# Head weights in two transfers of uneven shape, and a last weighing in another order, in a two-layer decode kernel

## The chip, the cores and the metric

The kernel runs on one core of a Trainium2 chip. The metric is device time in microseconds of one execution, as the median of several runs. Tensor, vector and scalar work run on TensorE (PE, with its weight loads as PEld), VectorE (DVE), ScalarE (ACT) and GpSimd (POOL); SyncE (SP) does nothing here but issue transfers. All transfers from memory run on the core's 16 DMA engines; each of them works through a ring of its own, in the order in which SP issued.

## The reference

One token for each of two batch entries goes twice through an attention block with cached keys and values and a gated FFN, all in 32-bit floats:

```python
B, D, H, Sk, Dh, F = 2, 448, 16, 4096, 256, 1792
def _A_ref(x, k_cache, v_cache, wq, wo):
    q = (x @ wq)                                    # per head: 448 -> 256
    scores = einsum("bhqd,bhkd->bhqk", q, k_cache) * Dh ** -0.5
    p = softmax(scores)
    o = einsum("bhqk,bhkd->bhqd", p, v_cache)
    return o.reshape(B, 1, H * Dh) @ wo
def _B_ref(x, W_gate, W_up, W_down):
    h = relu(x @ W_gate) * (x @ W_up)
    return h @ W_down
x = x + A(layernorm(x)); x = x + B(layernorm(x))
x = x + A(layernorm(x)); x = x + B(layernorm(x))    # the same weights and caches again
```

The caches are 128 MiB each for keys and values and are read for both layers; nearly all the bytes are theirs.

## The kernel before, in words

**Units and memory.** A unit is one head of one batch entry: 4 MB of keys and 4 MB of values, each cut into four pieces of 1 MB (`NC` = 4). The first attention goes through 32 units, the second through the same in reverse. Nearly all of on-chip memory is one `arena` of 27 slots of 1 MB: six blocks of four slots for keys and values, three single slots, mostly for head weights. Twenty-two pieces and one head that the first attention read last are kept for the second.

**Loads.** `loads`, `cut` and `grouped` write out one list of transfers (`pending`): per pair of units k, v, k, the next head's weights, v; then seven pieces of `w_in` and four of `w_out` for the FFN. `pump` issues them on SP in that order as soon as a slot is free; `release` frees a slot when its last product is recorded, and calls `pump`. In the middle, keys and values go as one transfer of 4 MB. Eight semaphores serve the transfers in turn, so that each issue also waits for the eighth transfer before it. A head's weights are one transfer of 128 rows of 7168 bytes: three stretches of 256 columns for rows 0 to 383 of wq, 128 columns that hold wq's last 64 rows (`TAIL`) for both halves of the head on the two halves of the partitions, and wo.

**Attention.** For a unit u, `score` multiplies each key piece by the query into the PSUM bank `raw`; `score_copy`, `score_turn`, `softmax_max` and `softmax_exp` make `probs`, with DVE, PE, POOL and ACT in turn; `weigh` multiplies each value piece by `probs` into `poa` or `pob`, in turn; `out_copy` (ACT) and `out_add` (DVE) make `row`; `out_turn` turns it with a product by ones, `out_keep` (DVE) stores it as `oT`, and `project` adds the head's share of the output to the bank `y`. `query` makes q for the next two units. PE runs what is recorded in the order of the code:

```python
for u in range(n_u - 1):
    scores(u)
    if u % 2: query(u + 1)
    if u < n_u - 2: outputs(u)
u = n_u - 1            # score, turn and softmax of the last unit, then:
outputs(u - 1)
out_turn(u - 1)
out_keep(u - 1)
outputs(u)             # weigh 0..3, softmax_sum, out_copy
```

`outputs(u)` is the four steps of `weigh`, `softmax_sum`, `out_copy` and, but for the last unit, `out_add`. `row` is one buffer: the last `out_copy` may write it only after the `out_turn` of the unit before. `busy(n, half)` issues n products of the identity with itself into a bank that nobody reads; they keep PE at work where it would wait.

**FFN.** `absorb` adds up `y` and turns it, `squares`, `deviation` and `inverse` make the layer norm's factor; `proj` goes through the pieces of `w_in` for gate and up, the loop over j through those of `w_out`, with one `busy` product behind some of them.

Of the kernel before, what the change touches and what calls it, by code (L numbers as in the profile page):

```python
# [14 lines left out]
B, D, H, S, DH, F = 2, 448, 16, 4096, 256, 1792  # L15
P = 128
DC = 5
FULL, TAIL = 3, 64
NT = S // P
CT = 8  # L20
UNIT = CT * DH
NC = NT // CT
BLOCKS, SINGLES = 6, 3
KEPT = 22
# [41 lines left out]
def two_layers(  # L66
# [3 lines left out]
    k_cache: bass.AP,  # L70
    v_cache: bass.AP,
    w_head: bass.AP,
    w_in: bass.AP,
    w_out: bass.AP,
    out: bass.AP,
):
    nc = tc.nc
# [34 lines left out]
    def pump():  # L112
        while pending:
            at = None
            for i, ((kind, name, c), n) in enumerate(pending[: AHEAD if pending[0][1] == 1 else 1]):
                if i and kind != "h":
                    continue
                last = at_of.get((kind, name, c - 1)) if kind in "kv" else None
                at = units.take(n, kind, last)
                if at is not None:  # L120
                    break
            if at is None:
                return
            pending.pop(i)
            src = source((kind, name, c), n)
            dst = arena[:, at * UNIT : at * UNIT + src.shape[1]]
            parts = [0, src.shape[1]]
            if kind == "v" and n == 1 and c == NC - 1 and name in (first[-1], second[-1]):
                parts[1:1] = [UNIT // 2]
            if not pending:  # L130
                parts[1:1] = [src.shape[1] - D]
            for i, j in zip(parts, parts[1:]):
                nc.sync.dma_start(dst[:, i:j], src[:, i:j])
            for k in range(n):
                at_of[kind, name, c + k] = at + k

    def get(*key):
        at = at_of[key]
        return arena[:, at * UNIT : (at + 1) * UNIT]

# [77 lines left out]
    xT = xr[:, :, :, 0]  # L218
# [18 lines left out]
    def busy(n, half):  # L237

        for _ in range(n):
            nc.tensor.matmul(  # L240
                po_all[half][:B, :DH], ident[:, :B],
                ident[:, None, :].to_broadcast([P, 2, P]), start=True, stop=True,
            )
# [47 lines left out]
    def attention(order, after):  # L291
# [8 lines left out]
        def query(u):  # L300
            h = order[u][0]
            w = get("h", h, 0)
            pq = pq_all
            for j in range(2):
                if j and u == 0:
                    again()
                for c in range(FULL):
                    at = c * DH + j * P
                    nc.tensor.matmul(  # L309
                        pq[:, j, :], w[:, at : at + P], xT[:, c, :], start=(c == 0), stop=False  # L310
                    )
                nc.tensor.matmul(  # L312
                    pq[:, j, :], w[:, FULL * DH : FULL * DH + P], xT[:, FULL + j, :],
                    start=False, stop=True,
                )
            q = q_pad[:, u // 2 % 2]
            nc.vector.tensor_copy(q[..., 1], pq)
            for v in (u, u + 1):
                q_of[v] = q[:, :, order[v][1]]
# [56 lines left out]
        def weigh(u, c):  # L376


            vt = get("v", order[u], c)
            if c == 0:  # L380
                po_of[u] = po_all[u % 2]
            for t in range(CT if u == n_u - 1 else 0):
                n = c * CT + t
                nc.tensor.matmul(
                    po_of[u][32 * (t % 4) : 32 * (t % 4) + 1, :DH],
                    p_of[u][:, n : n + 1],
                    vt[:, t * DH : (t + 1) * DH],
                    start=(c == 0 and t < 4),
                    stop=(c == NC - 1 and t >= 4),
                )  # L390
            for t in range(CT // 2 if u < n_u - 1 else 0):
                n = c * CT + 2 * t
                nc.tensor.matmul(  # L393
                    po_of[u][32 * t : 32 * t + 2, :],
                    p_of[u][:, n : n + 2],
                    vt[:, 2 * t * DH : (2 * t + 2) * DH],
                    start=(c == 0),
                    stop=(c == NC - 1),
                )
            if ("v", order[u], c) not in after:  # L400
                release("v", order[u], c)
            if u == n_u - 1 and 0 < c < NC - 1:
                busy(2, (u + 1) % 2)

        def out_copy(u):
            nc.scalar.activation(row[:, :DH], po_of[u][:, :DH], AF.Copy, scale=r_of[u][:, 0:1])  # L406
# [9 lines left out]
        def out_turn(u):  # L416
            pT_of[u] = ps_s.tile([P, 2], F32, name="small")
            for c in range(2):
                nc.tensor.matmul(  # L419
                    pT_of[u][:, c : c + 1], row[:, c * P : (c + 1) * P], ones,  # L420
                    start=True, stop=True,
                )

        def out_keep(u):
            h, b = order[u]
            if h not in oT_of:
                oT_of[h] = work.tile([P, 2, B], F32, name="oT")
            nc.vector.tensor_copy(oT_of[h][:, :, b], pT_of.pop(u))  # L428

        def project(u):  # L430
            h = order[u][0]
            if u % 2 == 0:
                return
            wo = get("h", h, 0)[:, FULL * DH + P :]
            for c in range(2):
                add(
                    c, oT_of[h][:, c, :], wo[:, c * D : (c + 1) * D],
                    start=(c == 1 and u == 1), stop=(u == n_u - 1),
                )
            if ("h", h, 0) not in after:  # L440
                release("h", h, 0)
            if u == n_u - 1:
                busy(1, 0)
# [24 lines left out]
        def outputs(u):  # L468
            for c in range(NC):
                weigh(u, c)  # L470
            softmax_sum(u)
            out_copy(u)
            out_add(u)
# [12 lines left out]
        softmax_max(u)  # L486
        softmax_exp(u)
        outputs(u - 1)
        out_turn(u - 1)
        out_keep(u - 1)  # L490
        outputs(u)
        busy(1, 0)
        out_turn(u)
        out_keep(u)
        project(u)

    def ffn(last):
# [65 lines left out]
        for j in range(4):  # L563
            w = get("out", "", j)
            first_k = (14 * j + 2) // 4
            for k in range(first_k, (14 * j + 16) // 4):
                w_k = w[:, (k - first_k) * D : (k - first_k + 1) * D]
                if last and k == 13:
                    for half in range(2):
                        n = D - DH if half else DH  # L570
                        nc.tensor.matmul(
                            y[32 * half : 32 * half + B, :n],
                            ident[64:, 64 + 32 * half : 64 + 32 * half + B],
                            yrow[64:, :n], start=False, stop=False,
                        )
                add(
                    0 if last and k > 10 else k % 2, stat[k], w_k, (y, other)[k % 2 if k <= 10 else 0],
                    start=(k == 1), stop=(k in ((9, 13) if last else (12, 13))),
                )
            release("out", "", j)  # L580
            if last and j == 2:
                nc.scalar.activation(yrow[64:], other[64:, :DH], AF.Copy)
            if j < 2 or not last:
                busy(1, 0)

    add(0, ident[:B, :B], row[:B, :D], start=True, stop=True)
    absorb()
# [14 lines left out]
def _arrays(np, A_x, A_k_cache, A_v_cache, A_wq, A_wo, B_W_gate, B_W_up, B_W_down, **_):  # L602

    rows = FULL * P
    wq = A_wq.reshape(D, H, DH)
    head = [wq[c * P : (c + 1) * P].transpose(1, 0, 2) for c in range(FULL)]
    head.append(wq[rows:].reshape(TAIL, H, 2, P).transpose(1, 2, 0, 3).reshape(H, P, P))
    wo = A_wo.reshape(H, 2, P, D)
    head += [wo[:, 0], wo[:, 1]]
    full = [w[c * P : (c + 1) * P] for w in (B_W_gate, B_W_up) for c in range(FULL)]  # L610
    full.insert(FULL, np.concatenate([B_W_gate[rows:], B_W_up[rows:]]))
    down = B_W_down.reshape(4, D, D)
    chunks = [down[j, m * P : (m + 1) * P] for j in range(4) for m in range(FULL)]
    chunks += [np.concatenate([down[j, rows:], down[j + 1, rows:]]) for j in (0, 2)]
    k = A_k_cache.reshape(B, H, P, 2, E, G, 2, P).transpose(0, 1, 7, 3, 6, 5, 4, 2)
    found = {
        "x": A_x,
        "k_cache": k.reshape(B, H, P, S * 2),
        "v_cache": A_v_cache,
        "w_head": np.concatenate(head, axis=2),  # L620
        "w_in": np.stack(full),
        "w_out": np.concatenate(chunks, axis=1),
    }
    return {n: np.ascontiguousarray(a) for n, a in found.items()}
# [24 lines left out]
```

## Time and profile before

| | |
|---|---|
| median of 3 runs | 1327.57 us (1326.64 to 1327.68) |
| the profiled execution | 1328.09 us, its span 1326.3 us |
| mean granted TensorE clock | 0.761 |
| bytes moved | 562.42 MB, mean 424 GB/s |
| PE busy, PEld, DVE, ACT, POOL | 956.7, 322.8, 134.8, 92.0, 47.7 us |

The span runs from the first instruction to the last; the execution's own time holds 1.8 us more. A DMA share of 1.00 is all 16 engines at work; it can come out a little over 1 in a short stretch, since the records of two rows overlap by some nanoseconds. The first attention goes to about 670 us, the first FFN to 691, the second attention to 1305, the last FFN to the end.

### The profile page before, as it was taken

To read this page: it belongs to the slowest core of one execution; us is meant where nothing else is said; L and a number is where in the kernel's file an instruction comes from. 1 tells how busy PE (TensorE), PEld (TensorE's weight loads), DVE (VectorE), ACT (ScalarE), POOL (GpSimd) and SP (SyncE) were. 2 spreads that over 40 slices of the span, in tenths; PEclk is the share of its full clock that TensorE was granted. 3 is DMA by queue.
4 is the path that set the end of the run, shared out by engine and by line. 5 is a ranking of instruction groups with operands and counts; after the bars stand their busy time and mean duration, and the time that the engine had idled before them with its cause. 6 is when DMAs were issued, how large, how long until landed. Compare 5 with 4: busy or idle time off the path is not lost.

```text
span 1326.3 us, 13786 instructions
## 1 busy us (share of the span) xinstructions
PE 956.7 (72%) x6076; PEld 322.8 (24%) x6076; DVE 134.8 (10%) x457; ACT 92.0 (7%) x280; POOL 47.7 (4%) x134
## 2 busy tenths in 40 slices
PE   4767677877777766767788867777676676766678
PEld 2222123231232212222243322222122221222213
DVE  1101011010110100000101111010010100101100
ACT  1000000000000000000011100000000000000001
POOL 0000000000000000000000000000000000000000
PEclk9777766667767777686798897776777777778779
DMA  9999999999999999999999999999999999999997
GB/s 403 427 433 428 432 428 436 425 434 426 427 436 430 430 429 426 434 428 432 421 368 391 434 431 430 432 429 431 430 430 429 432 428 433 429 432 430 428 423 324
DMA packets 28152, 562.42 MB, mean 424 GB/s; under 512 B 3126, under 2 KB 3260, under 8 KB 10556
## 3 DMA queue, kind: packets, MB, share of 16 engines
q1 hardware_dynamic: 28084, 561.53, 99.1%
q8 instruction: 48, 0.79, 0.2%
q14 instruction: 12, 0.10, 0.0%
q10 hardware_dynamic: 8, 0.01, 0.0%
HBM read 561.52 MB, written 0.00 MB: 423 GB/s over the span
## 4 chain that ended last, share of the span: by engine, by line
PE 63%; another core or an unknown queue 19%; DMA 10%; DVE 3%; issue 2%; ACT 1%; POOL 0%; POOLq 0%; SPq 0%; ACTq 0%; DVEq 0%
PE rawb L333 12%; PE pob L393 12%; PE rawa L333 12%; PE poa L393 12%; PE small L347 5%; PE pq L309 4%; DMA arena<-in_k_cache_dram 3%; DMA arena<-in_v_cache_dram 3%; PE small L419 3%; DVE found_s L341 3%; DMA arena<-in_w_in_dram 2%; DMA arena<-in_w_out_dram 2%; PE pq L312 1%; PE y L249 0%
## 5 line engine op out<-in xcount | busy, mean ns | idle before, releaser
L333 PE MATMUL rawb<-arena,q_pad 128*2 128x512 f32 x1024 | 181.6, 846 | 96.6 <-DMA arena<-in_k_cache_dram 96.6
L333 PE MATMUL rawa<-arena,q_pad 128*2 128x512 f32 x1024 | 174.5, 814 | 96.2 <-DMA arena<-in_k_cache_dram 95.7
L393 PE MATMUL poa<-arena,probs 128*2 128x512 f32 x1024 | 172.9, 838 | 74.7 <-DMA arena<-in_v_cache_dram 51.2
L393 PE MATMUL pob<-arena,probs 128*2 128x512 f32 x960 | 173.1, 886 | 38.4 <-DMA arena<-in_v_cache_dram 38.3
L347 PE MATMUL small<-ident,found_s 128*128 128x8 f32 x512 | 73.5, 270 | 36.6 <-DVE found_s L341 36.4
L347 PEld LDWEIGHTS small<-ident,found_s 128*128 128x128 f32 x512 | 67.7, 206 | 99.6 <-DVE found_s L341 99.6
L393 PEld LDWEIGHTS poa<-arena,probs 128*2 128x2 f32 x1024 | 31.5, 106 | 187.6 <-issue 144.5
L333 PEld LDWEIGHTS rawb<-arena,q_pad 128*2 128x2 f32 x1024 | 24.1, 96 | 194.7 <-DMA arena<-in_k_cache_dram 121.6
L333 PEld LDWEIGHTS rawa<-arena,q_pad 128*2 128x2 f32 x1024 | 24.3, 94 | 190.4 <-issue 179.7
L361 ACT ACTIVATE nm<-top,nsr 128x1 f32<-128x1 f32 x64 | 18.8, 294 | 718.7 <-POOL top L356 718.7
L419 PEld LDWEIGHTS small<-ones,row 128*128 128x128 f32 x256 | 44.3, 246 | 91.7 <-issue 80.4
L393 PEld LDWEIGHTS pob<-arena,probs 128*2 128x2 f32 x960 | 28.7, 109 | 155.0 <-issue 154.8
L356 POOL PARTITION_ALL_REDUCE top<-mx x64 | 22.5, 351 | 1165.5 <-DVE mx L354 1152.0
L309 PE MATMUL pq<-xs,arena 128*128 128x2 f32 x384 | 62.3, 278 | 0.0
L309 PEld LDWEIGHTS pq<-xs,arena 128*128 128x128 f32 x384 | 58.9, 229 | 2.6 <-issue 1.3
L419 PE MATMUL small<-ones,row 128*128 128x1 f32 x256 | 49.7, 298 | 2.6 <-DVE row L411 2.2
L428 DVE COPY oT<-small 128x2 f32<-128x2 f32 x64 | 10.2, 160 | 361.0 <-PE small L419 361.0
L411 DVE SCALAR_TENSOR_TENSOR row<-pob,ri,row 128x256 f32<-128x256 f32 x30 | 14.5, 484 | 206.5 <-ACT row L406 206.5
L411 DVE SCALAR_TENSOR_TENSOR row<-poa,ri,row 128x256 f32<-128x256 f32 x32 | 15.5, 484 | 186.9 <-ACT row L406 186.9
L406 ACT ACTIVATE row<-pob,ri 128x256 f32<-128x256 f32 x32 | 15.1, 473 | 244.1 <-PE pob L393 231.0
L341 DVE COPY found_s<-rawb 128x512 f32<-128x512 f32 x32 | 22.1, 692 | 90.9 <-PE rawb L333 90.9
L341 DVE COPY found_s<-rawa 128x512 f32<-128x512 f32 x32 | 22.1, 692 | 70.0 <-PE rawa L333 70.0
(81 smaller groups left out, 314.6 us busy)
## 6 DMA issues: line engine op xcount, KB each, us to landing
arena<-in_k_cache_dram SPq DMA_DIRECT2D x59, 4096.0 KB, 54.5
arena<-in_v_cache_dram SPq DMA_DIRECT2D x58, 4096.0 KB, 55.3
arena<-in_w_head_dram SPq DMA_DIRECT2D x31, 896.0 KB, 55.0
arena<-in_w_in_dram SPq DMA_DIRECT2D x14, 896.0 KB, 16.4
arena<-in_v_cache_dram SPq DMA_DIRECT2D x12, 1024.0 KB, 12.1
arena<-in_k_cache_dram SPq DMA_DIRECT2D x8, 1024.0 KB, 13.7
arena<-in_w_out_dram SPq DMA_DIRECT2D x4, 896.0 KB, 16.8
arena<-in_v_cache_dram SPq DMA_DIRECT2D x4, 512.0 KB, 47.6
```

The source lines that it names most:

```text
L309: nc.tensor.matmul(pq[:, j, :], w[:, at : at + P], xT[:, c, :], start=(c == 0), stop=False)
L312: nc.tensor.matmul(pq[:, j, :], w[:, FULL * DH : FULL * DH + P], xT[:, FULL + j, :], start=False, stop=True,)
L333: nc.tensor.matmul(raw[u % 2][32 * g : 32 * g + 2, :], q_of[u][:, j, 1 - half : 3 - half], kt[:, g, :], start=(c == 0), stop=(c == NC - 1),)
L341: nc.vector.tensor_copy(found_s, raw[u % 2])
L347: nc.tensor.matmul(s[:, :, e, :], found_s[:, e * P : (e + 1) * P], pick, start=True, stop=True,)
L356: nc.gpsimd.partition_all_reduce(mx_of[u], mx, P, RED.max)
L361: nc.scalar.activation(nm, mx_of.pop(u), AF.Copy, scale=nsr[:, b : b + 1])
L393: nc.tensor.matmul(po_of[u][32 * t : 32 * t + 2, :], p_of[u][:, n : n + 2], vt[:, 2 * t * DH : (2 * t + 2) * DH], start=(c == 0), stop=(c ...
L406: nc.scalar.activation(row[:, :DH], po_of[u][:, :DH], AF.Copy, scale=r_of[u][:, 0:1])
L411: nc.vector.scalar_tensor_tensor(row[:, :DH], po_of.pop(u)[:, DH:], r_of[u][:, 1:2], row[:, :DH], op0=ALU.mult, op1=ALU.add,)
L419: nc.tensor.matmul(pT_of[u][:, c : c + 1], row[:, c * P : (c + 1) * P], ones, start=True, stop=True,)
L428: nc.vector.tensor_copy(oT_of[h][:, :, b], pT_of.pop(u))
```

## The change

It has two parts.

*Head weights.* The transfer of a head's weights loses the 128 columns with wq's tail: 128 rows of 6656 bytes, 832 KB. Ahead of it SP issues a second one of 64 KB: eight rows of 8192 bytes (they lie 8448 bytes apart in memory), each of which fills eight partitions with 1 KB, so that wq's last 64 rows lie on the first 64 partitions behind the rest of the head. `query` multiplies those 64 partitions alone.

*Last weighing.* The two pairs of unread products between the steps of the last `weigh` go. The turn of the unit before comes after the second step of the last weighing instead of ahead of the first. An unread product is added between the last `out_turn` and `out_keep`, and in the first FFN one more behind the last piece of `w_out`.

```diff
+HEAD = FULL * DH + 2 * D
...
+            if kind == "h":
+                nc.sync.dma_start(
+                    arena[:TAIL, at * UNIT + HEAD : at * UNIT + HEAD + DH],
+                    w_tail[name, :, : 8 * DH].rearrange("e (r n) -> e r n", n=DH),
+                )
             parts = [0, src.shape[1]]
...
+                at = HEAD + j * P
                 nc.tensor.matmul(
-                    pq[:, j, :], w[:, FULL * DH : FULL * DH + P], xT[:, FULL + j, :],
+                    pq[:, j, :], w[:TAIL, at : at + P], xT[:TAIL, FULL, :],
                     start=False, stop=True,
                 )
...
-            if u == n_u - 1 and 0 < c < NC - 1:
-                busy(2, (u + 1) % 2)
...
-            wo = get("h", h, 0)[:, FULL * DH + P :]
+            wo = get("h", h, 0)[:, FULL * DH :]
...
         outputs(u - 1)
-        out_turn(u - 1)
-        out_keep(u - 1)
-        outputs(u)
+        for c in range(NC):
+            weigh(u, c)
+            if c == 1:
+                out_turn(u - 1)
+                out_keep(u - 1)
+        softmax_sum(u)
         busy(1, 0)
+        out_copy(u)
         out_turn(u)
+        busy(1, 0)
         out_keep(u)
         project(u)
...
             if j < 2 or not last:
-                busy(1, 0)
+                busy(2 if j == 3 else 1, 0)
...
-    head.append(wq[rows:].reshape(TAIL, H, 2, P).transpose(1, 2, 0, 3).reshape(H, P, P))
+    tail = np.zeros((H, 8, 8 * DH + 64), A_wq.dtype)
+    tail[:, :, : 8 * DH] = wq[rows:].transpose(1, 0, 2).reshape(H, 8, 8 * DH)
```

PE at the end of the first attention, before: the last values of the unit before (`poa`), its turn (L419), and the last weighing (L384) with the unread products of L240 in it.

```order
L393 MATMUL poa<-arena,probs 2x512 x16
L419 MATMUL small<-ones,row 128x1 x2
L384 MATMUL pob<-arena,probs 1x256 x16
L240 MATMUL poa<-ident 2x256 x2
L384 MATMUL pob<-arena,probs 1x256 x8
L240 MATMUL poa<-ident 2x256 x2
L384 MATMUL pob<-arena,probs 1x256 x8
L240 MATMUL poa<-ident 2x256
L419 MATMUL small<-ones,row 128x1 x2
L249 MATMUL y<-arena,oT 2x256
```

The same place after the change (the last weighing is now L392, the turn L425, the unread product L247).

```order
L401 MATMUL poa<-arena,probs 2x512 x16
L392 MATMUL pob<-arena,probs 1x256 x16
L425 MATMUL small<-ones,row 128x1 x2
L392 MATMUL pob<-arena,probs 1x256 x16
L247 MATMUL poa<-ident 2x256
L425 MATMUL small<-ones,row 128x1 x2
L247 MATMUL poa<-ident 2x256
L256 MATMUL y<-arena,oT 2x256
```

The first half of the last weighing has moved ahead of the turn, four unread products are gone, and one stands behind the second turn.

SP in the first attention, before: one stretch of the list from a head's weights to the next, where DMAHW are the eight semaphores of the transfers and PE is the product that frees a slot.

```order
L133 DMA arena<-in_w_head_dram 128x1792 [waits PE_49]
L133 DMA arena<-in_v_cache_dram 128x8192 [waits DMAHW0_49,PE_49]
L133 DMA arena<-in_k_cache_dram 128x8192 [waits DMAHW1_49,PE_49]
L133 DMA arena<-in_v_cache_dram 128x8192 [waits DMAHW3_49,DMAHW2_49,PE_49]
L133 DMA arena<-in_k_cache_dram 128x8192 [waits DMAHW4_49,PE_49]
L133 DMA arena<-in_w_head_dram 128x1792 [waits PE_49]
```

The same stretch after.

```order
L130 DMA arena<-in_w_tail_dram 64x1x256 [waits DMAHW2_49]
L140 DMA arena<-in_w_head_dram 128x1664 [waits DMAHW3_49,PE_49]
L140 DMA arena<-in_v_cache_dram 128x8192 [waits DMAHW4_49,PE_49]
L140 DMA arena<-in_k_cache_dram 128x8192 [waits DMAHW5_49,PE_49]
L140 DMA arena<-in_v_cache_dram 128x8192 [waits DMAHW6_49,PE_49]
L140 DMA arena<-in_k_cache_dram 128x8192 [waits DMAHW7_49,PE_49]
L130 DMA arena<-in_w_tail_dram 64x1x256 [waits DMAHW0_49]
```

Each head now takes two of the eight semaphores, so that six transfers stand between a head and the next where there were five.

More of the change, by code (lines that the diff above doesn't have):

```diff
@@ L72, in two_layers @@
     w_head: bass.AP,
+    w_tail: bass.AP,
     w_in: bass.AP,
@@ L620, in _arrays @@
         "w_head": np.concatenate(head, axis=2),
+        "w_tail": tail,
         "w_in": np.stack(full),
```

## The prediction

> **What bounds the kernel now.** The page comes first: its totals by DMA and the row of slices.
>
> ```profile
> span 1326.3 us, 13786 instructions
> DMA  9999999999999999999999999999999999999997
> GB/s 403 427 433 428 432 428 436 425 434 426 427 436 430 430 429 426 434 428 432 421 368 391 434 431 430 432 429 431 430 430 429 432 428 433 429 432 430 428 423 324
> q1 hardware_dynamic: 28084, 561.53, 99.1%
> q8 instruction: 48, 0.79, 0.2%
> ```
>
> The 16 DMA engines are busy in all forty slices and move about 430 GB/s. Only slices 20 and 21 (the first FFN) and the last one are thin: at 430, a slice of 33.2 us loses 4.8, 3.0 and 8.2 us there. PE at 72% is no bound. So I read the two thin places only, and first the chain of waits at the end.
>
> ```profile
> 1289.21 16.43 DMA arena<-in_w_in_dram
> ...
> 1305.71 15.75 DMA arena<-in_w_out_dram
> ...
> 1321.50 1.02 PE y L249 x7
> ...
> 1323.62 0.38 ACT found_s L593
> ```
>
> From 1289 on the chain is transfers; PE adds 2 us behind the last. What the last weighing costs there (it runs near 1300) is therefore not on the path. Next, the DMA share us by us at that end, then at the first FFN (columns: stretch, its length, PE, PEld, DVE, ACT, POOL busy, granted clock, DMA share, GB/s).
>
> ```profile
> 1316.00:1317.00 1.00, 0.79 (x8) 0.80 (x8) 0.07 (x1) 0.00 (x0) 0.00 (x0) 1.00 0.80 324
> 1317.00:1318.00 1.00, 1.00 (x18) 0.68 (x21) 0.19 (x1) 0.00 (x0) 0.00 (x0) 1.00 0.65 265
> 1318.00:1319.00 1.00, 1.00 (x22) 0.47 (x14) 0.00 (x0) 0.00 (x0) 0.00 (x0) 1.00 0.50 208
> 1319.00:1320.00 1.00, 1.00 (x10) 0.34 (x4) 0.00 (x0) 0.00 (x0) 0.00 (x0) 1.00 0.48 194
> 1320.00:1321.00 1.00, 0.94 (x16) 0.45 (x16) 0.00 (x0) 0.00 (x0) 0.00 (x0) 1.00 0.44 176
> 1321.00:1322.00 1.00, 0.94 (x16) 0.37 (x8) 0.00 (x0) 0.38 (x1) 0.00 (x0) 1.00 0.16 56
> ```
>
> ```profile
> 668.00:669.00 1.00, 0.82 (x6) 0.31 (x4) 0.00 (x0) 0.47 (x1) 0.00 (x0) 1.00 0.80 330
> ...
> 670.00:671.00 1.00, 0.82 (x9) 0.27 (x3) 0.00 (x0) 0.47 (x2) 0.00 (x0) 1.00 0.55 229
> ...
> 672.00:673.00 1.00, 0.85 (x12) 0.36 (x16) 0.42 (x3) 0.00 (x0) 0.00 (x0) 1.00 0.29 102
> 673.00:674.00 1.00, 1.00 (x16) 0.32 (x12) 0.00 (x0) 0.00 (x0) 0.00 (x0) 1.00 0.00 0
> 674.00:675.00 1.00, 1.00 (x16) 0.39 (x12) 0.00 (x0) 0.00 (x0) 0.00 (x0) 1.00 0.75 115
> ```
>
> This is the observation that matters. All transfers here spread 128 rows evenly over 16 engines, yet the engines do not finish together. At the end the first is out of work at about 1316.5; by 1319 half are; the share then stays at 0.44 to 0.50, that is seven or eight engines, until they stop between 1321 and 1322. So eight engines run 3.5 to 5.5 us late and eight 0 to 2.4 us. The lost shares add up to 0.20 + 0.35 + 0.50 + 0.52 + 0.56 + 0.84 = 3.0 us, what perfect balance would be worth. At 668 to 673.3 the same spread of 4.8 us ends the first half, falling more evenly: one or more of the earlier engines are some 3 us late too. What makes engines late is instruction loading: 48 blocks of 16 KB go through the same engines (q8), some 24 in each half. If eight engines take them, that is three each and some 1.5 us per block.
>
> **The change part by part.** *The last weighing at the first FFN.* The chain there:
>
> ```profile
> 654.78 6.42 PE poa L393 x32
> ...
> 661.22 0.48 ACT row L406
> ...
> 662.87 1.84 PE pob L384 x32
> 664.71 0.63 PE poa L240 x3
> ...
> 666.41 0.65 PE poa L240 x3
> ...
> 668.23 0.48 ACT row L406
> ...
> 672.15 2.50 PE rawa L509 x24
> 674.67 7.40 DMA arena<-in_w_in_dram
> ...
> 683.12 6.64 DMA arena<-in_w_out_dram
> ```
>
> The next-to-last weighing ends at 661.2, and PE waits for ACT, DVE and the turn until the last begins at 662.8. With the turn put behind its second step that wait (1.6 us) goes and the turn costs 0.5. The unread products of L240 take 0.86 each time (664.71 to 665.55 and 666.41 to 667.28): 1.7 less. Together 2.8 us earlier. The added product behind the turn runs while DVE copies oT: nothing. But the last weighing also needs its values. The late engines end their last transfer before the stall at 673.3; the four w_in transfers of 0.92 MB queued behind the values need 0.92/0.425 = 2.16 us each, so the values landed at about 664.6. PE at 668.2 - 2.8 = 665.4 is just behind that. So 0.8 us more of lateness is free, and each further one takes from the 2.8.
>
> *The tail transfer.* Each head's 896 KB become 832 KB in 128 rows and 64 KB in eight rows of 8 KB. Bytes stay the same. Price of a row, from two quiet stretches (packets, MB, share of 16 engines):
>
> ```profile
> q1 hardware_dynamic: 80, 2.59, 100.1%
> q1 hardware_dynamic: 270, 1.71, 101.9%
> ```
>
> The first is 520 to 526: 79 rows of 32 KB, 1.001 x 16 x 6 / 79 = 1.216 us each. The second is 678 to 682: 238 rows of mostly 7 KB and 32 completions, 1.019 x 16 x 4 / 238 = 0.274 us. The line through both has 0.942 us for 25,600 bytes (27 GB/s an engine) and 0.01 us for the row itself. A 6656-byte row then takes 0.255, 0.019 less: eight of them save an engine 0.15 us per head. An engine with one tail row writes it as eight pieces of 1 KB: 8 x 0.048 = 0.38, or 0.31 if it goes as one 8-KB row; net +0.16 to +0.24 per head. I take +0.20, since recorded rows overlap by a few ns (shares over 100%). No view shows a DMA of eight rows; the nearest is the load of x.
>
> ```profile
> q10 hardware_dynamic: 8, 0.01, 0.0%
> ```
>
> Two rows in and two out left eight packets, four of data and four completions, so a DMA of two rows ran on two engines; eight rows should run on eight. [...]
>
> So the change is a shift: per head eight engines +0.20, the other eight -0.15. The question is whether the late eight are the ones relieved. No view names the engines. [...] I give that 0.8.
>
> *At the end.* Thirteen heads are loaded after the stall near 700. Late eight: 5.5 - 13 x 0.15 = 3.5. Early eight: the latest, 2.4, becomes 2.4 + 13 x 0.20 = 5.0 (4.5 to 5.5). The last engine is now 5.0 behind instead of 5.5: **-0.5 us** (-1.0 to 0). The balance overshoots; most of the 3.0 stays unwon.
>
> *At the first FFN.* Sixteen heads lie before it. Late eight 4.8 - 2.4, plus 0.4 since SP issues the first tail before the first head: 2.8. Early eight: 3.2 + 16 x 0.20 = 6.4. The last engine is 1.5 us later than now; so the values land at 666.1, the last weighing ends near 666.6 instead of 668.0, and PE's chain keeps 1.5 of the 2.8. The next w_in is issued when the first is used up:
>
> ```profile
> 673.17 1.08 SPq L133 DMA_DIRECT2D arena<-in_w_in_dram  x2
> ```
>
> ```profile
> arena<-in_w_in_dram SPq DMA_DIRECT2D x1, 896.0 KB, 4.6
> ```
>
> Issued at 673.17, it lands 4.6 us later, at 677.7. Issued 1.5 us earlier it would land at 676.3 on the early engines, but the latest engine is free only at 673.3 + 1.5 = 674.8 and needs 2.16 more: 677.0. From there to 689.8 the chain is transfers, one behind the other. **-0.8 us** (-2.4 if the spread is milder, +0.2 with 0.24 per head).
>
> *SP's queue.* Thirty-one more issues. SP takes
>
> ```profile
> 657.19 0.33 SPq L133 DMA_DIRECT2D arena<-in_w_in_dram  x1
> ```
>
> 0.33 us each, and every DMA waits for the eighth before it, so each tail takes one of eight places in flight. Behind it v and k queue. With 55 us from issue to landing some 45 us of work is in the rings then; a v issued 5 to 7 us later starves nothing. Cover gone, it would cost those 5 us a head. I take 0.
>
> *The second unread product after the first FFN.* PE idles 0.63 us there; 0.43 fits: nothing. It may matter by the clock:
>
> ```profile
> 694.00:696.00 2.00, 2.00 (x12) 1.57 (x12) 0.00 (x0) 0.00 (x0) 0.00 (x0) 0.62 1.05 437
> 696.00:698.00 2.00, 1.74 (x10) 0.38 (x10) 0.17 (x1) 0.00 (x0) 0.00 (x0) 0.50 0.99 414
> 698.00:700.00 2.00, 2.00 (x14) 0.76 (x14) 0.33 (x2) 0.93 (x2) 0.00 (x0) 0.50 0.58 147
> 700.00:702.00 2.00, 2.00 (x16) 0.34 (x12) 0.17 (x1) 0.82 (x2) 0.00 (x0) 0.67 0.85 352
> ```
>
> The granted clock is 0.50 from about 694.5 to 701.3 while the first scores run, and the DMA share falls to 0.58 and 0.85: 1.1 us of all engines. At full clock these scores, and the transfers they release, come up to 2 us earlier. Bounds 0 to -2; I take 0, because the stretch before holds mostly small products with or without one more.
>
> *Sum.* -0.8 - 0.5 = -1.3 us on the profiled execution, whose own time of 1328.09 is 0.5 above the median of the runs shown, 1327.57: **1326.2 us**.
>
> **The rivals.** *The late eight get the tail.* Then the first half ends 3.2 later (4.8 + 16 x 0.20 = 8.0) and the second 2.6. At the FFN the weighing's gain is used up by landings and w_in comes 0.7 later: 0.7 + 2.6 = 3.3, **1330.9**, slower. [...]
>
> *The FFN gains nothing.* Landings on the latest engine, or a clock of 0.50 once the unread products are gone (the 2.50 us of L509 then double), eat the 0.8 and part of the rest: **1327.2**.
>
> *Both places gain in full.* The early engines' lateness is milder than read and the scores after the FFN run at full clock: -2.4 - 0.8 - 1 = **1323.4**.
>
> *Each small DMA costs its fixed part in the stream.* Against it: w_in's 0.92 MB pieces ran at 423 GB/s, so starting a DMA is hidden. If it weren't, at the 2 us that may lie between issue and data (issue at 673.17, data in the row from 674), 31 tails cost **62 us**, 1389. [...]
>
> **How the numbers follow.** Forecast 0.46 (own range 1323.6 to 1328.6); late eight hit 0.16; nothing at the FFN 0.19; both in full 0.18; fixed cost 0.01. The range 1322.6 to 1331.2 takes in all but the last and the rim of the others. A measurement of this kernel tells about 0.2%, 2.65 us, from no change. Faster than 1324.9: 0.15 of "in full", 0.14 of the forecast, 0.02 else: 0.31. Slower than 1330.2: 0.12 of the late-eight case, 0.03 each of the forecast and the FFN rival, 0.01: 0.19. Same 0.50.
>
> **What would show it.** Right: the DMA share at the end falls less early and reaches half later; 31 DMAs of 64 KB with eight packets of 1 KB per engine; the last weighing begins under 0.1 us after the one before; w_in's next issue 1 to 2 us earlier relative to the last landing. Wrong: a share that stays near 0.5 for 6 to 8 us at the end (late eight hit), a flat fall to zero within 2 us (balance better than read), or a clock of 0.50 between 667 and 675.

## The result and the profile after

The changed kernel takes **1347.39 us** in the median (1346.26 to 1348.93), beside 1327.62 us for the kernel before: a ratio of 1.0152 with a 95% interval of 1.014 to 1.0164, so 20 us slower. The forecast was 1326.2 us and its range ended at 1331.2. The profiled execution after took 1347.64 us.

The same rows of the page after (leaving out the first slice, slices 19 to 21 counted from 0, and the last two, the slices before hold 425 to 436 GB/s, those now 418 to 430):

```profile
span 1345.9 us, 13826 instructions
GB/s 396 426 421 426 425 428 427 427 420 424 427 426 423 419 425 426 425 426 418 422 345 409 422 429 428 427 422 430 420 428 426 419 428 419 427 429 419 424 420 283
q1 hardware_dynamic: 30316, 561.53, 98.8%
q8 instruction: 47, 0.77, 0.2%
```

Not only the two thin places changed: the whole stream is slower. A long stretch of the second attention, before and then after (columns as in the prediction's stretches, the last two are DMA share and GB/s):

```profile
720.00:1250.00 530.00, 379.96 (x2409) 119.63 (x2401) 54.45 (x176) 33.84 (x109) 19.80 (x54) 0.76 1.00 430
```

```profile
720.00:1250.00 530.00, 385.46 (x2411) 131.32 (x2403) 53.34 (x177) 33.89 (x109) 19.80 (x54) 0.75 1.01 425
```

The engines are as busy as before, at 1.00, and move 425 GB/s instead of 430. The same 561.53 MB take 1306 us at 430 and 1321 us at 425: 15 of the 20 us. So the rows themselves became slower. Where, two stretches tell, one with a head's weights in it and one between two heads. Before:

```profile
402.00:410.00 8.00, 3.68 (x26) 0.75 (x19) 0.48 (x1) 0.47 (x1) 0.00 (x0) 0.86 1.02 434
410.00:443.00 33.00, 25.44 (x155) 8.23 (x159) 3.52 (x12) 2.00 (x7) 1.47 (x4) 0.72 1.00 429
```

and after:

```profile
405.00:417.00 12.00, 8.13 (x48) 1.37 (x48) 0.88 (x3) 1.24 (x4) 0.42 (x2) 0.72 1.01 407
417.00:446.00 29.00, 17.55 (x136) 7.28 (x136) 3.43 (x12) 2.00 (x7) 1.47 (x4) 0.85 1.00 431
```

Between heads nothing changed (429 and 431); around a head the rate falls to 407. In these 12 us that is 24/431 x 12 = 0.7 us for one head, one of the dearer ones: the row records of single heads give 0.3 to 0.7 us. The trace's packet records, which give the start, the size and the duration of every row, show it microsecond by microsecond. For rows that start in each microsecond after the change: their number, and by how many ns their mean lies above that of undisturbed rows (46, 253 and 1213 ns for 1024, 6656 and 32,768 bytes):

```
us     1024 B     6656 B      32768 B
408    -          12: +6       5: +5
409     8: +0     19: +9      12: +45
410    16: +0     17: +17     10: +137
411    14: +0     12: +42      6: +214
412    10: +4     13: +74      8: +230
413    16: +3     15: +80      9: +200
414    -          11: +28      9: +27
415    -           7: +5      12: +6
```

The tail's own 1-KB rows are not held up: 47.5 ns in the mean of all of them, 46 undisturbed. The long rows that run at the same time are held up, by up to 230 ns in the mean of a microsecond, and only then. They lie on all sixteen engines, on those with tail rows as on those without. Below are two rings at this head, followed from row to row (each starts 3 to 6 ns before the one ahead of it ends; KB and ns, in order, without the 4-byte completions):

```
no tail   6.5 KB x8: 253 256 256 282 268 261 254 289   32 KB: 1408 1446 1306 1218 1221
tail      32 KB: 1214 1258 1304   1 KB x8: 46 each   6.5 KB x8: 328 351 285 326 271 354 382 309   32 KB: 1225
```

Added up in this way over 27 of the heads, about half of the lost time lies on the eight engines without tail rows and half on the long rows of the eight with them.

The end after the change, against the table of the end before:

```profile
1331.00:1332.00 1.00, 0.99 (x10) 0.17 (x2) 0.00 (x0) 0.00 (x0) 0.00 (x0) 1.00 0.93 385
...
1333.00:1334.00 1.00, 1.00 (x10) 0.17 (x2) 0.20 (x1) 0.00 (x0) 0.00 (x0) 1.00 0.78 319
1334.00:1335.00 1.00, 0.57 (x5) 0.46 (x5) 0.42 (x1) 0.00 (x0) 0.00 (x0) 1.00 0.63 249
1335.00:1336.00 1.00, 1.00 (x11) 0.68 (x14) 0.19 (x1) 0.00 (x0) 0.00 (x0) 0.62 0.34 138
...
1338.00:1339.00 1.00, 1.00 (x12) 0.34 (x11) 0.00 (x0) 0.00 (x0) 0.00 (x0) 0.67 0.12 48
1339.00:1340.00 1.00, 1.00 (x18) 0.45 (x15) 0.00 (x0) 0.00 (x0) 0.00 (x0) 1.00 0.08 30
```

The share falls from 0.93 to nothing over 9 us instead of 5.5, and for the last four microseconds one to three engines work alone, not seven or eight. From 1329 to 1340 (the microseconds between those shown included) the lost shares add up to 4.9 us, 1.9 more than before.

### The profile page after: what moved, and what is told of

It reads as the page before. It is cut to its first block, busy times and chain, and to the rows that moved or that the text cites. A ratio compares the mean times of both kernels' runs of the same rounds, so it can differ in the third digit from the quotient of the medians.

```text
span 1345.9 us, 13826 instructions
## 1 busy us (share of the span) xinstructions
PE 957.4 (71%) x6066; PEld 324.7 (24%) x6066; DVE 132.8 (10%) x457; ACT 92.1 (7%) x280; POOL 47.7 (4%) x134
## 3 DMA queue, kind: packets, MB, share of 16 engines
q1 hardware_dynamic: 30316, 561.53, 98.8%
## 4 chain that ended last, share of the span: by engine, by line
PE 52%; another core or an unknown queue 21%; DMA 21%; DVE 3%; issue 2%; ACT 1%; POOL 0%; SPq 0%; POOLq 0%; ACTq 0%; DVEq 0%
PE rawa L341 10%; PE pob L401 10%; PE rawb L341 10%; PE poa L401 9%; DMA arena<-in_v_cache_dram 7%; DMA arena<-in_w_head_dram 7%; PE small L355 4%; DMA arena<-in_k_cache_dram 4%; PE pq L316 3%; DMA arena<-in_w_in_dram 3%; PE small L425 3%; DVE found_s L349 2%; PE pq L320 1%; PE y L256 1%
## 5 line engine op out<-in xcount | busy, mean ns | idle before, releaser
L425 PEld LDWEIGHTS small<-ones,row 128*128 128x128 f32 x256 | 44.2, 245 | 88.6 <-issue 81.1
L425 PE MATMUL small<-ones,row 128*128 128x1 f32 x256 | 49.6, 298 | 0.4 <-ACT row L412 0.4
```

The source lines that it names most:

```text
L425: nc.tensor.matmul(pT_of[u][:, c : c + 1], row[:, c * P : (c + 1) * P], ones, start=True, stop=True,)
```

## The experiments

The seven kernels below ran beside the kernel before, whose median was 1328.02 us (7 runs) for the first four and 1327.29 us (21 runs) for the last three. Short diffs are against the kernel after unless said otherwise, and leave out what only follows from them (mostly the layout in memory). The theory that these stretches suggested: the tail lands on eight engines with eight 1-KB pieces each (the trace has 1984 such rows and 248 completions more than before, so 64 and eight for each of the 31 tails), and its engines write to places to which, in a transfer of 128 rows, other engines write; two engines at one place hold each other up. The places and the meeting are the author's assumption: no packet record names an engine or a partition. Rivals: rows of 6656 bytes are slow by themselves; a second small transfer per head holds up the rings wherever it writes; everything is late engines.

**Heads alone.** The kernel after with the last weighing as it was before.

```diff
-        for c in range(NC):
-            weigh(u, c)
-            if c == 1: ...turn...
+        out_turn(u - 1)
+        out_keep(u - 1)
+        outputs(u)
```

> Only the head part of the change: tail transfer of eight rows and rows of 6656 bytes, with the last weighing as before. If the head transfers cost all of the 20 us: 1347 to 1349. If the new order of the last weighing costs a part: that part less, 1328 if all of it.

Measured: 1347.33 us (2 runs; ratio 1.0141, 1.0093 to 1.0189). So the head weights carry the loss, which these two runs put at 12 to 25 us.

**No tail.** Rows of 6656 bytes, no second transfer; the query leaves out wq's last 64 rows.

```diff
-                nc.sync.dma_start(arena[:TAIL, ...], w_tail[name, ...])
...
-                nc.tensor.matmul(pq[:, j, :], w[:TAIL, at : at + P], ...)
```

> The changed kernel without the tail transfers and without the two products that use them (the last 64 rows of wq are left out of q); the rows of 6656 bytes stay. Theory A (the eight-row transfers disturb the other engines while they run, because each of their engines writes where other engines write): 1322 to 1326, since 2 MB less are moved. Theory B (rows of 6656 bytes are slow by themselves; in the trace they took 0.284 us instead of 0.253): 1328 to 1336. Theory C (31 more issues and semaphores): 1322 to 1326 as A.

Measured: 1320.98 us (ratio 0.9948, 0.9922 to 0.9975). The 2 MB less are worth 4.7 us at 430 GB/s, the rest of the 7.0 lies within the weighing's gain and the scatter of these runs (1320.24 to 1324.1). Rows of 6656 bytes took 260 ns in the mean, rows of 32 KB 1218.7 as before (1218.9). Rows of 6656 bytes aren't slow by themselves.

**Tail in groups of four partitions.** Two transfers of eight rows of 4 KB, each row on four partitions: row e of the first fills partitions 4e to 4e+3, row e of the second 32+4e to 32+4e+3.

```diff
-                nc.sync.dma_start(
-                    arena[:TAIL, at * UNIT + HEAD : at * UNIT + HEAD + DH],
-                    w_tail[name, :, : 8 * DH].rearrange("e (r n) -> e r n", n=DH),
-                )
+                for i in range(2):
+                    nc.sync.dma_start(
+                        arena[32 * i : 32 * i + 32, at * UNIT + HEAD : at * UNIT + HEAD + DH],
+                        w_tail[name, i, :, : 4 * DH].rearrange("e (r n) -> e r n", n=DH),
+                    )
```

> The same bytes on the same eight engines, but as two transfers of eight rows of 4 KB per head, each row filling four partitions, the first transfer partitions 0 to 31, the second 32 to 63. [...] Theory B: 1345 to 1349. Theory C (number of transfers): 1350 to 1370, as there are now 62 added ones.

Measured: 1333.2 us (5 runs; ratio 1.004, 1.0023 to 1.0056): 14 of the 20 us are gone, with one transfer more per head, the same bytes, again eight engines and the same 1-KB pieces. The stretch around a head:

```profile
402.00:414.00 12.00, 7.62 (x46) 1.44 (x39) 0.48 (x1) 0.47 (x1) 0.00 (x0) 0.78 1.01 429
```

It is back at 429 GB/s. What is left over shows at the first FFN, in slices 20 and 21 (330 and 408 GB/s against 368 and 391 before, 1.7 us at 430), and at the end:

```profile
GB/s 388 428 427 431 430 429 430 433 426 429 427 435 428 432 426 430 431 431 429 419 330 408 434 430 430 430 432 428 429 430 428 431 430 429 431 430 428 431 421 299
1321.00:1322.00 1.00, 0.99 (x10) 0.17 (x2) 0.36 (x1) 0.00 (x0) 0.00 (x0) 1.00 0.87 357
1322.00:1323.00 1.00, 0.59 (x6) 0.62 (x6) 0.27 (x1) 0.00 (x0) 0.00 (x0) 1.00 0.69 276
1323.00:1324.00 1.00, 1.00 (x15) 0.68 (x19) 0.18 (x1) 0.00 (x0) 0.00 (x0) 1.00 0.35 140
...
1325.00:1326.00 1.00, 1.00 (x14) 0.39 (x7) 0.00 (x0) 0.00 (x0) 0.00 (x0) 1.00 0.16 65
1327.00:1328.00 1.00, 0.94 (x17) 0.32 (x9) 0.00 (x0) 0.30 (x1) 0.00 (x0) 1.00 0.11 36
```

From 1324 on two to four engines work alone; the shares lost from 1318 to 1328 add up to 4.8 us, against 3.0 before. This run also tells which engines are late, since its tails land on eight engines alone and so mark them in the landing records of the transfers next to them (near 1206 the tail's eight landings each come 0.2 us behind one of the sixteen of the transfer ahead). By how many us each engine is behind the first of all sixteen, on the w_in transfer that lands at 1308:

```
without a tail  0.0  0.2  3.1  4.2  4.5  4.6  4.7  4.8
with a tail     5.0  5.1  5.5  5.9  6.8  7.6  9.4  9.8
```

From one head to the next the tail engines fall behind by 0.35 to 0.41 us (7.41, 7.76, 8.17 us for the last of them near 1184, 1206 and 1247). Thirteen times 8 x 47.5 ns = 0.38 is 4.9 us; without it they would be at 0.0, 0.2, 0.6, 1.0, 1.9, 2.6, 4.4 and 4.8.

**64 rows of 1 KB.** The same bytes and partitions in 64 rows, four for each of 16 engines if they are shared evenly.

```diff
-                    w_tail[name, :, : 8 * DH].rearrange("e (r n) -> e r n", n=DH),
+                    w_tail[name, :, :DH]
```

> The tail as one transfer of 64 rows of 1 KB, which should be spread over all 16 engines, four partitions each. [...] Theory B: 1340 to 1347. Theory C: 1347 as now.

Measured: 1340.43 us (ratio 1.0089, 1.006 to 1.0118). The engines finish as they did before (5.7 us apart on the last transfer, 5.5 before), so no shift is seen, yet the hold-up stays: 425 GB/s in the long stretch, 6656-byte rows at 290.5 ns.

```profile
720.00:1250.00 530.00, 376.88 (x2388) 123.19 (x2389) 53.57 (x177) 33.41 (x108) 19.91 (x54) 0.77 1.01 425
```

An even load does not end it. That the time lies just inside theory B's range does not speak for B: without a tail the 6656-byte rows took 260 ns.

**The same groups on the upper partitions.** The two transfers of eight rows of 4 KB of the run in groups, to partitions 64 to 95 and 96 to 127, against that run:

```diff
-                        arena[32 * i : 32 * i + 32, at * UNIT + HEAD : ...],
+                        arena[TAIL + 32 * i : TAIL + 32 * i + 32, at * UNIT + HEAD : ...],
...
-                    pq[:, j, :], w[:TAIL, at : at + P], xT[:TAIL, FULL, :],
+                    pq[:, j, :], w[TAIL:, at : at + P], xT[TAIL:, FULL + 1, :],
```

> The same two transfers of eight 4-KB rows as in the run in groups of four partitions, with the same engines, pieces and bytes, but on partitions 64 to 95 and 96 to 127 (the query reads them there). [...] Rival (what cost time was that one engine's eight pieces span two places of four partitions, or that rows of 8 KB were cut in eight): this run has neither, and takes the 1333 of the run in groups, with 6656-byte rows at 263 ns.

Measured: 1350.95 us (ratio 1.018, 1.0163 to 1.0197), 18 us more than in groups below, and not the 1333 of the rival. The stretch around a head, and the long one:

```profile
407.00:419.00 12.00, 7.15 (x40) 1.03 (x32) 0.48 (x1) 0.47 (x1) 0.00 (x0) 0.64 1.02 410
```

```profile
720.00:1250.00 530.00, 387.96 (x2420) 133.50 (x2412) 53.33 (x177) 33.83 (x109) 19.81 (x54) 0.75 1.01 424
```

Nothing that the code or a record shows of the transfers differs from the run in groups but the partitions, and each lands on eight engines as there. This is the run that decides: neither the number of transfers, nor the size of rows and pieces, nor the number of engines, but the place written to. (That they are the same eight engines in both runs, no record says.)

**The tail as 128 rows of 512 bytes.** The old layout, 128 columns on 128 partitions, as a transfer of its own.

```diff
-                    arena[:TAIL, at * UNIT + HEAD : at * UNIT + HEAD + DH],
-                    w_tail[name, :, : 8 * DH].rearrange("e (r n) -> e r n", n=DH),
+                    arena[:, at * UNIT + HEAD : at * UNIT + HEAD + P], w_tail[name, :, :P]
...
-                    pq[:, j, :], w[:TAIL, at : at + P], xT[:TAIL, FULL, :],
+                    pq[:, j, :], w[:, HEAD : HEAD + P], xT[:, FULL + j, :],
```

> wq's last 64 rows in the old layout (128 columns on 128 partitions), but as a transfer of its own of 128 rows of 512 bytes beside the 128 rows of 6656. [...] Theory (place, and the shift onto eight engines, are what costs): no hold-up, no shift; only the overhead of the rows: a 1-KB row took 46 ns where 1 KB in a long row is 38, so 8 ns x 8 rows x 31 heads = 2 us more than before, 1329 to 1331.5; 6656-byte rows at 253 to 260 ns. Rival (a second small transfer of each head holds up the ring, wherever it writes): as the run with 64 rows of 1 KB or more, 1338 to 1341, with 6656-byte rows near 290 ns.

Measured: 1329.58 us (9 runs; ratio 1.0017, 1.0008 to 1.0027). With 31 transfers more, 32,548 packets instead of 28,084, and the weighing of the kernel after.

```profile
720.00:1250.00 530.00, 373.85 (x2404) 119.31 (x2400) 54.41 (x176) 33.89 (x109) 19.80 (x54) 0.77 1.01 430
```

No hold-up: 430 GB/s, and the 6656-byte rows took 263.7 ns. No shift: the shares lost at the end, from 1317 to 1323, add up to 2.9 us, 3.0 before. The small rows took 27.3 ns each.

**The weighing alone.** The kernel before with the edits of the last weighing and of the unread products.

```diff
-            if u == n_u - 1 and 0 < c < NC - 1:
-                busy(2, (u + 1) % 2)
...
-        out_turn(u - 1)
-        out_keep(u - 1)
-        outputs(u)
+        for c in range(NC): weigh(u, c); if c == 1: ...turn...
...
-                busy(1, 0)
+                busy(2 if j == 3 else 1, 0)
```

> The kernel before with the edits of the last weighing and of the unread products alone; heads as before in one transfer. Theory (the gap at the first FFN follows PE's chain, 2.8 us shorter, until the last values land about 0.8 us before PE now gets there): 0.8 to 2.4 us less in front of the first FFN, nothing at the end: 1325.2 to 1327.2, and the first w_in behind the stall issued 1 to 2.4 us earlier. Rival (landing or a lower clock takes the place of PE's chain): 1327.5 to 1328.5, no change.

Measured: 1326.18 us (11 runs), ratio 0.9991 with an interval of 0.998 to 1.0002: 1.1 us less, as expected in size, but not told apart from no change. PE in time at the first FFN (start, length, what, idle time before with its cause), first before:

```profile
662.80 1.91 PE L384 MATMUL pob<-arena,probs 128*1 128x256 f32 x32
...
672.15 3.21 PE L509 MATMUL rawa<-arena,xs 128*32 128x448 f32 x32 [0.27 <-DVE xs L265]
...
682.12 0.96 PE L509 MATMUL rawb<-arena,xs 128*32 128x448 f32 x8 [0.80 <-DMA arena<-in_w_in_dram]
...
691.47 0.83 PE L260 MATMUL pq<-halves,found_s 128*128 128x4 f32 x6 [0.63 <-ACT found_s L254]
```

and with the weighing alone:

```profile
659.91 1.91 PE L384 MATMUL pob<-arena,probs 128*1 128x256 f32 x32
662.29 1.74 PE L384 MATMUL pob<-arena,probs 128*1 128x256 f32 x24
664.68 0.61 PE L384 MATMUL pob<-arena,probs 128*1 128x256 f32 x8 [0.65 <-DMA arena<-in_v_cache_dram]
...
669.39 2.78 PE L512 MATMUL rawa<-arena,xs 128*32 128x448 f32 x24 [0.27 <-DVE xs L265]
...
679.94 0.96 PE L512 MATMUL rawb<-arena,xs 128*32 128x448 f32 x8 [0.81 <-DMA arena<-in_w_in_dram]
...
690.00 0.83 PE L260 MATMUL pq<-halves,found_s 128*128 128x4 f32 x6
```

The FFN's first product starts 2.8 us earlier, the last of w_in 2.2 us, and the FFN ends 1.5 us earlier. The last quarter of the weighing now waits for its values, at 664.68. No other kernel here that loads all the weights was faster in the median.

## Why the prediction was wrong

*Where the 20 us are.* Means of the packet records, in ns, and the medians (the kernel before that ran beside each took 1327.3 to 1328.0 us):

```
                        tail rows   6656 B   32768 B    us (median)
before                      -         -      1218.9     1327.6
128 rows of 512 B          27.3     263.7    1218.7     1329.6
groups of four             47.5     263.2    1218.6     1333.2
64 rows of 1 KB            49.9     290.5    1225.6     1340.4
after                      47.5     284.2    1227.6     1347.4
groups, upper partitions   49.0     296.0    1227.1     1351.0
```

Against the groups of four, the kernel after has 3968 rows that are 21.0 ns longer and 14,976 that are 9.0 ns longer: over 16 engines 5.2 + 8.4 = 13.6 us for each. The two times differ by 14.2. The shift of load onto eight engines costs some 3 to 4 us: groups of four against 128 rows, 3.6 between the medians and 2.9 when each is set against the kernel before that ran beside it, though these two differ by one transfer per head as well. The 128 rows cost 2.3 us over before as run beside them; if the weighing's 1.1, which is not clear of the noise, is in it, 3.4 for 31 transfers and their rows. The row records give about the same, 3.5: 6.8 us per engine for the small rows and 0.3 for the completions, less 3.6 for the shorter head rows.

*Bounds and the late engines.* The two thin places were read rightly, and so was the lateness before: on the w_in transfer that lands near 1308, eight engines are 0 to 2.5 us and eight 3.5 to 5.6 us behind the first. That eight engines take the tail was right (eight completions for each). Which eight take it, no run shows by number, and so none shows the 0.8; the run in groups of four shows where most late ones are: six of the eight engines without a tail are 3.1 to 4.8 us behind the first. The term "early eight: the latest, 2.4" was mis-sized. Two engines of the tail's eight are late too, 4.4 and 4.8 us. On these the shift is added: by the forecast's own sum the latest comes to 4.8 + 13 x 0.20 = 7.4 us and not 5.0, so 1.9 us later than the 5.5 of before, where -0.5 stood. The groups of four show it without the hold-up: the end loses 4.8 us of all engines instead of 3.0. The two sets that the 0.8 was to tell apart are not disjoint; the forecast treated late and early as two blocks, which the even fall of the share at 668 to 673 already spoke against. A block of instructions does make its ring some 1.5 us late, as estimated: one near 1112.5 took 1.07 us, and the 32-KB row behind it 1.71 instead of 1.22. The sums hold but for 0.1 us in two places: 6.4 - 4.8 is 1.6, not 1.5, and 677.7 - 677.0 is 0.7, not 0.8.

*The weighing.* Right alone in its steps: 2.8 us earlier on PE, stopped at the values at 664.6. In the median it gave 1.1 us, not clear of no change, where 0.8 stood for the kernel after. In the kernel after the values land much later. Its first FFN product starts only 0.8 us before that of the run with the heads alone (680.98 against 681.78), and the medians of the two show nothing of it:

```profile
675.02 0.61 PE L392 MATMUL pob<-arena,probs 128*1 128x256 f32 x8 [0.17 <-DMA arena<-in_v_cache_dram]
676.27 0.61 PE L392 MATMUL pob<-arena,probs 128*1 128x256 f32 x8 [0.64 <-DMA arena<-in_v_cache_dram]
...
680.98 2.74 PE L520 MATMUL rawa<-arena,xs 128*32 128x448 f32 x24 [0.27 <-DVE xs L272]
```

*The tail's price: the step that failed.* Its own rows were priced well (47.5 ns against 48; 253 undisturbed for a 6656-byte row against 255). But "+0.16 to +0.24 per head" held the tail's rows and the shorter head rows alone, and gave the tail no effect on the long rows around it. That effect, put at nothing, is 13.6 us over 31 heads, 0.44 us per head on each of the 16 engines, more than 0.24, the top of the range. The only load of a few rows in the trace of before, that of x at 1.7 us, ran with no full stream beside it (DMA share 0.56 from 1 to 2 us) and could not show it. No term and no rival had this mechanism; all rivals below 62 us ended by 1330.9.

The partitions written to decide whether there is a hold-up: 6656-byte rows took 263 to 264 ns in the groups of four on the lower partitions and in the 128 rows, and 284 to 296 with eight partitions for each row, in the 64 rows and in the groups on the upper partitions. Half of the lost time lay on the eight engines without tail rows. Why the partitions decide, why the hold-up reaches those eight engines, and whether two engines meet at one place at all, no run here shows.

*SP's queue, fixed cost.* A tail issue took 0.62 us in the median, nearly twice the assumed 0.33:

```profile
L130 SPq DMA_DIRECT2D arena<-in_w_tail_dram x31: 618/619/787, 0.7 to 1214.1; - x31
```

It starved nothing, as forecast: the share stays at 1.00 between heads. The rival of 62 us is out: 31 transfers more cost 2.3 to 3.4 us in the 128 rows. No run shows its 2 us between issue and data: in the trace of before the first row came at 674.13, 0.96 us after the issue at 673.17.

## What to carry to other kernels

The bytes of a small transfer into part of the partitions were not its price: 64 KB for each of 31 heads cost each engine 13.6 us in the longer rows around them, and the same two transfers 18 us more on one half of the partitions than on the other (1350.95 and 1333.2 us). So look at what it does to the rows beside it, and try it on other partitions. Here the share stayed at 1.00 to 1.01 while the rate fell from 430 to 425 GB/s: the rows had become slower, and the packet records around that moment told which. Before load is shifted from late engines to early ones, mark each engine: the latest of the early ones decides (4.8 us here, where 2.4 was taken), not the group.

## What the runs showed of the hardware that was not expected

- While eight engines write 64 KB in 1-KB rows, eight rows each, 32-KB rows take up to 230 ns more than 1213 in the mean of a microsecond, over some 5 us and on all sixteen engines. The 1-KB rows stay at 47 to 50 ns in every layout.
- Moving the same two transfers from partitions 0 to 63 to 64 to 127 cost 18 us in 31 heads (1333.2 to 1350.95), 0.57 us each.
- Thirty-one more transfers of 128 rows of 512 bytes into a full stream cost 0.07 to 0.11 us each.
